# Another order of all engines' steps, with the first two masks on VectorE and g in the raw w_out

## The chip, the cores and the metric

The kernel runs on one core of one Trainium2 chip. The metric is the device time of one execution in microseconds (us). Engines are named as in the profile: PE (TensorE matmuls), PEld (its weight loads), DVE (VectorE), ACT (ScalarE), POOL (GpSimd) and SP (SyncE, which issues the transfers here).

## The reference

Attention over 8 batches, 8 heads, 576 positions and 64 head dimensions, followed by a feed-forward stage over 4608 tokens of 512 values. Each attention output is the sum of two: one on q, k and v averaged over groups of four positions, repeated four times, and one local, in which a position sees only those less than four away.

```
mask = np.abs(pos[:, None] - pos[None, :]) < factor        # factor = 4
out_d = sm_attn(q_d, k_d, v_d)                             # q_d = mean of 4 positions, ...
out_up = np.repeat(out_d, factor, axis=2)
scores = scale * np.matmul(q, k.transpose(0, 1, 3, 2))
scores = np.where(mask, scores, -1000000000.0)
out_local = np.matmul(softmax(scores), v)
x = out_up + out_local                                     # -> (4608, 512)

h = x @ w_in                                               # 512 -> 1024
solu = h * softmax(h)
ln = (solu - mean) / np.sqrt(var + 1e-06) * g_ln
out = ln @ w_out                                           # 1024 -> 512
```

Inputs are float32, the weights float64.

## The kernel before, in words

**Tiles.** The feed-forward stage takes 36 tiles of 128 tokens. A tile i goes through `xhl` (x is split into a rounded high part xh and a low part xl), `ffn_in` (h in two halves of 12 matmuls, line 862: xh with wi_h and wi_l, xl with wi_h; then the maximum `nmx` L870, the exponential L874, the product `e` L877, the mean, the centring L900 or L902, and the write of u to memory), `ffn_back` (u is read back as v, in blocks), `ffn_ut` (two block transposes of v on DVE, L963, then the split into uh on ACT, L969, and ul, L972) and `ffn_out` (o in two halves of 12 matmuls, L986, scaled on ACT, L993, and stored). The last tile, 35, is transposed by PE (`ut`, L959) instead of going through memory. The accumulators of h and of o exist once each: h_(i+1) starts when `e` of tile i has been computed, and o_(i+1) when o_i has been scaled.

**Attention.** A batch is prepared (`prepare`): for batches 0 and 1 q and k are transposed by PE (`qp`, `kp`, L557) and copied (L265, or L263 on ACT); for the others DVE transposes them (L463, L467). DVE sums groups of four into qd and kd (L419). Then there are four `Pooled` units (per pair of heads: scores `sd` L788, maximum L795, exponential, division L812, transpose `pdt` L823, product `po` L844, addition to x L578) and five windows of local attention: `Local` units for batches 0 to 2 and the last window of the others, `PairOfLocals` for the rest. A `Local` unit computes scores `sc` (L607), masks them, subtracts the maximum, exponentiates, divides (L639 to L645), transposes (`plt` L655), multiplies with v (`xp` L665) and adds to x.

**Masks.** In `Local`, a batch below MASKED (2 before) is masked by PE: two bf16 matmuls of the identity with the mask (L600) start the accumulation that the score matmuls continue; DVE then takes the maximum (L620) and subtracts it (L622) straight from the scores. Any other batch is masked by DVE (L625 adds the mask), DVE takes the maximum (L630), and POOL or DVE subtracts it (L632).

**Weights.** They come as float64, as sixteen pieces of 512 KB: 0 to 7 of w_in, 8 to 15 of w_out. A piece is turned into float32 by an absolute value on ACT (L364), a clip on POOL or DVE (L366), and a shift and two combining steps on DVE (L370, L375, L379). It is then rounded into a high part on ACT and a low part. For w_out, `G_LATE` multiplies g in at the rounding (L402) and again in the low part, a fused DVE step (L404).

**Order.** All these steps are numbered in a list `plan`. ORDER is a written-out order of those numbers, by which the instructions of all engines are issued; each engine and the SP queue of transfers runs its own in that order. OTHER lists the steps that go to the second of two engines (POOL or DVE, ACT or DVE). 24 `warm` steps of two matmuls on an idle tile (L1043) are spread over the first part of ORDER.

```
if early:
    for a in range(2):
        nc.tensor.matmul(sc[:, a, ...], ident_b, mask_b..., start=True, stop=False)
...
if early:
    nc.vector.tensor_reduce(out=mx, in_=sc, op=ALU.max, axis=AX.X)
    nc.vector.tensor_tensor(out=pl, in0=sc, in1=max_bc, op=ALU.subtract)
else:
    nc.vector.tensor_tensor(out=pl, in0=sc, in1=mask..., op=ALU.add)
    nc.vector.tensor_reduce(out=mx, in_=pl, op=ALU.max, axis=AX.X)
    engine(nc.gpsimd, nc.vector).tensor_tensor(out=pl, in0=pl, in1=max_bc, op=ALU.subtract)
```

Of the kernel before, what the change touches and what calls it, by code (L numbers as in the profile page):

```python
# [137 lines left out]
def pooled_local_attention_then_solu_ffn(  # L138
# [40 lines left out]
    MASKED = 2  # L179
    WARM = 24  # L180
    SUMS_ON_PE = 0
    G_LATE = True
# [973 lines left out]
```

## Time and profile before

| | |
|---|---|
| median of 3 runs | 602.21 us (599.0 to 603.77) |
| the profiled execution | 600.81 us |
| its span, first to last instruction | 599.0 us |
| mean granted clock of TensorE | 0.996 |
| busy: PE, DVE, ACT, POOL | 567.2, 487.0, 330.7, 285.2 us |
| moved | 99.57 MB, 166 GB/s over the span |
| PE in h (L862) and o (L986), share of the chain that ended last | 25% and 27% |

A row of a group gives line, engine, operation, tiles with shapes and count, then busy time and the mean of one in ns, then the idle time of the engine before these instructions and what ended it. A row of a timeline gives start, duration, engine, line and tiles, and in brackets the idle time before. A matmul's end is modelled, so what a matmul costs PE in a row of them is read from start to start.

### The profile page before, as it was taken

How to read it: one execution, taken by the hardware profiler on the slowest of the kernel's cores; microseconds unless marked ns; L12 is line 12 of the kernel's file. 1: busy time of each engine (PE TensorE's matmuls, PEld its weight loads, DVE VectorE, ACT ScalarE, POOL GpSimd, SP SyncE). 2: the span in 40 equal slices, each digit the busy share in tenths (PEclk: the TensorE clock that was granted, in tenths of full speed). 3: DMA queues.
4: the chain of work that ended last, by engine and by line, in shares of the span. 5: the costliest groups of instructions: out<-in, count | busy, mean ns of one | idle time of the engine just before them, and what ended most of it. 6: DMA issues, size and time to landing. Idle time of an engine off the chain costs nothing.

```text
span 599.0 us, 15199 instructions
## 1 busy us (share of the span) xinstructions
PE 567.2 (95%) x5852; PEld 434.6 (73%) x5852; DVE 487.0 (81%) x792; ACT 330.7 (55%) x743; POOL 285.2 (48%) x433
## 2 busy tenths in 40 slices
PE   6887878999999999999989999999999999999996
PEld 3565556777777777777767877777777777778874
DVE  6999999988988889878897997998788568645540
ACT  4667657267654576456563665456635764243542
POOL 4567577653554666363552155446325643322120
PEclk9999999899999999999999999999999999999999
DMA  8998756778678876887986878776474442332330
GB/s 267 264 224 223 169 130 116 184 161 182 170 194 175 199 172 161 209 178 178 219 175 175 162 194 206 167 177 194 124 202 136 128 148 89 108 135 86 112 124 35
DMA packets 207111, 99.57 MB, mean 166 GB/s; under 512 B 163136, under 2 KB 193344, under 8 KB 207040
## 3 DMA queue, kind: packets, MB, share of 16 engines
q1 hardware_dynamic: 207040, 98.61, 65.4%
q8 instruction: 46, 0.75, 0.5%
q14 instruction: 25, 0.20, 0.1%
HBM read 65.54 MB, written 27.79 MB: 156 GB/s over the span
## 4 chain that ended last, share of the span: by engine, by line
PE 64%; DVE 13%; DMA 7%; issue 4%; POOL 4%; SPq 4%; ACT 3%; DVEq 0%; POOLq 0%; ACTq 0%
PE o L986 27%; PE h L862 25%; PE po L844 2%; PE sd L788 2%; DMA w<-in_moe_w_in_dram 2%; DMA vw<-in_v_dram 2%; DMA qm<-in_q_dram 1%; PE pdt L823 1%; SPq L286 1%; PE xp L753 1%; SPq L305 1%; PE sc L695 1%; PE xp L665 1%; DVE nmx L870 1%; POOL w L366 1%
## 5 line engine op out<-in xcount | busy, mean ns | idle before, releaser
L986 PE MATMUL o<-wo_h,uh 128*128 128x512 f32 x288 | 118.4, 411 | 1.9 <-ACT osb L993 1.6
L862 PE MATMUL h<-wi_h,xh 128*128 128x512 f32 x288 | 115.9, 402 | 1.4 <-DVE e L877 1.2
L862 PE MATMUL h<-wi_h,xl 128*128 128x512 f32 x288 | 114.2, 397 | 0.7 <-POOL xl L1020 0.7
L986 PE MATMUL o<-wo_l,uh 128*128 128x512 f32 x288 | 114.7, 398 | 0.0
L862 PE MATMUL h<-wi_l,xh 128*128 128x512 f32 x288 | 113.6, 394 | 0.0
L986 PE MATMUL o<-wo_h,ul 128*128 128x512 f32 x288 | 79.2, 396 | 1.5 <-POOL ul L972 0.9
L874 ACT ACTIVATE e<-h,nmx 128x1024 f32<-128x1024 f32 x36 | 40.1, 1114 | 53.7 <-DVE nmx L870 53.2
L986 PEld LDWEIGHTS o<-wo_h,uh 128*128 128x128 f32 x288 | 54.5, 189 | 18.6 <-issue 2.8
L870 DVE TENSOR_REDUCE nmx<-h 128x1 f32<-128x1024 f32 x36 | 43.7, 1214 | 29.3 <-PE h L862 29.3
L862 PEld LDWEIGHTS h<-wi_h,xh 128*128 128x128 f32 x288 | 54.0, 188 | 15.6 <-DVE e L877 1.6
L986 PEld LDWEIGHTS o<-wo_h,ul 128*128 128x128 f32 x288 | 54.0, 188 | 15.6 <-DVE ul L972 1.4
L862 PEld LDWEIGHTS h<-wi_h,xl 128*128 128x128 f32 x288 | 54.1, 188 | 14.7 <-POOL xl L1020 1.5
L986 PEld LDWEIGHTS o<-wo_l,uh 128*128 128x128 f32 x288 | 54.7, 190 | 11.8
L862 PEld LDWEIGHTS h<-wi_l,xh 128*128 128x128 f32 x288 | 54.1, 188 | 12.3
L972 POOL TENSOR_TENSOR ul<-v,uh 128x512 fp32r<-128x512 f32 x31 | 40.1, 1299 | 46.4 <-ACT uh L969 37.1
L969 ACT ACTIVATE uh<-v 128x512 fp32r<-128x512 f32 x70 | 43.3, 623 | 29.7 <-DVE v L963 19.9
L877 DVE SCALAR_TENSOR_TENSOR e<-h,e 128x1024 f32<-128x1024 f32 x36 | 43.7, 1214 | 18.0 <-ACT e L874 17.7
L963 DVE STREAM_TRANSPOSE v<-v 128x512 f32<-128x512 f32 x70 | 46.9, 689 | 0.8 <-DMA v<-u 0.7
L993 ACT ACTIVATE osb<-o,s 128x512 f32<-128x512 f32 x36 | 24.5, 680 | 35.6 <-PE o L986 22.2
L882 POOL TENSOR_SCALAR nmu<-su 128x1 f32<-128x1 f32 x36 | 9.3, 257 | 70.3 <-DVE e L877 63.5
L900 ACT ACTIVATE e<-e,nmu 128x1024 f32<-128x1024 f32 x28 | 32.1, 1146 | 16.8 <-POOL nmu L882 16.8
L919 ACT ACTIVATE e<-e 128x1024 f32<-128x1024 f32 x35 | 36.7, 1049 | 2.2 <-DMA u<-e 2.2
(125 smaller groups left out, 1124.6 us busy)
## 6 DMA issues: line engine op xcount, KB each, us to landing
u<-e SPq DMA_DIRECT2D x35, 512.0 KB
v<-u SPq DMA_DIRECT2D x140, 128.0 KB
vs<-in_v_dram SPq DMA_DIRECT2D x32, 288.0 KB
out_dram<-osb SPq DMA_DIRECT2D x36, 256.0 KB
qm<-in_q_dram SPq DMA_DIRECT2D x96, 72.0 KB
km<-in_k_dram SPq DMA_DIRECT2D x96, 72.0 KB
vw<-in_v_dram SPq DMA_DIRECT2D x80, 64.0 KB
vw<-in_v_dram SPq DMA_DIRECT2D x40, 128.0 KB
```

What stands on the lines that cost most here:

```text
L788: nc.tensor.matmul(sd[rows((par + c) % 2), (0, 2, 1)[c], :], qd_flat[rows(par), (NPR - 1 - pr) * SD + c * QN:][:, 0:64], bt.kd[rows(par), ...
L862: nc.tensor.matmul(hps[:, n, :], src[:, cc, :], wt[:, cc, n * 512:(n + 1) * 512], start=(cc == 0 and src is xh and wt is wi_h), stop=(cc = ...
L870: nc.vector.tensor_reduce(out=nmx, in_=hf, op=ALU.max, axis=AX.X, negate=True)
L874: nc.scalar.activation(e, hf, AF.Exp, bias=nmx, scale=1.0, accum_out=se)
L877: nc.vector.scalar_tensor_tensor(out=e, in0=hf, scalar=1.0, in1=e, op0=ALU.mult, op1=ALU.mult, accum_out=su)
L900: nc.scalar.activation(e, e, AF.Identity, bias=nmu, scale=1.0)
L919: nc.scalar.activation(e0, e, AF.Square, accum_out=m2)
L963: nc.vector.transpose(vg, vg)
L969: nc.scalar.activation(uh, tp, AF.Copy)
L972: (usual if v is None else engine(usual, nc.vector)).tensor_tensor(out=ul, in0=tp, in1=uh.bitcast(F32), op=ALU.subtract)
L986: nc.tensor.matmul(o, src[:, j, :], wt[:, 4 * g + j, :], start=(g == 0 and j == 0 and src is uh and wt is wo_h), stop=(g == 1 and j == 3 a ...
L993: nc.scalar.activation(osb, o, AF.Copy, scale=s)
```

## The change

Three constants change, and with them the tables.

```diff
 ORDER = """
-8 0 23 168 169 22 170 171 172 173 174 25 24 10 175 160 161 162 163 164 176 177 16 26 27 32 28
...
+23 16 165 166 2 4 167 168 169 170 171 24 26 27 25 28 29 3 172 33 32 30 31 173 174 197 17 175
...
 OTHER = """
-37 53 59 93 178 186 202 210 242 250 258 266 274 282 471 482 524 541 543 549 566 568 574 643 671
...
+27 78 188 215 220 239 255 276 292 294 437 551 553 576 609 628 651 685 697 709 721 731 738 752
...
     EARLY = 2
-    MASKED = 2
+    MASKED = 0
     WARM = 24
     SUMS_ON_PE = 0
-    G_LATE = True
+    G_LATE = False
     FIRST_ON_PE = ()
```

MASKED = 0 lets all `Local` units of batches 0 and 1 take the branch that the others took: no mask matmuls, the mask added by DVE, and one step more each (ten in all), the subtraction, on POOL or DVE. The matrices ident_b and mask_b are gone, and the warm-up matmuls use a zeroed tile `filler` that POOL writes. G_LATE = False multiplies g into the float32 piece of w_out by an ACT step of its own, after which the piece is rounded and its low part taken as for w_in, on POOL or DVE:

```
nc.scalar.activation(t, t, AF.Copy, scale=g)
...
nc.scalar.activation(hi, t, AF.Copy)
yield
engine(nc.gpsimd, nc.vector).tensor_tensor(out=lo, in0=t, in1=hi.bitcast(F32), op=ALU.subtract)
```

Lines of the changed file are one lower than before (L624 is the old L625). OTHER has 115 entries, not 133. By its and ORDER's doing DVE has, over the whole program: 13 clips, not 6; four low parts of weights, and no fused ones (8); 20 mask adds of `Local`, not 10; 9 xl, not 19; 35 ul, not 41; 8 pairs of sums of v, not 10; 2 wide subtractions and 2 wide multiplications of `PairOfLocals`, not 3 and 4. What DVE gives up of these goes to POOL. In the SP queue the first transfers are a piece of w_in, q, k, k, q, and the second piece, where they were a piece, k, q, and the second piece.

The first scores on PE, before: `sc_1` and `sc_2` are windows 1 and 2 of batch 0.

```order
L823 MATMUL pdt_0_406<-ident,pd_0_318 72x64 x12
L600 LDWEIGHTS ident_b
L600 MATMUL sc_1_422<-mask_b,ident_b 128x256
L600 LDWEIGHTS ident_b
L600 MATMUL sc_1_422<-mask_b,ident_b 128x256
L607 MATMUL sc_1_422<-kT_171,qT_170 64x64 x16
```

And now, where windows 0 and 1 come first:

```order
L606 MATMUL sc_0_378<-kT_151,qT_150 64x64 x16
L606 MATMUL sc_1_395<-kT_151,qT_150 64x64 x16
L822 MATMUL pdt_0_412<-ident,pd_0_246 72x64 x12
L1042 LDWEIGHTS filler
L1042 MATMUL warm_442<-filler 128x512
```

Each unit's pair of mask matmuls is gone, and the score matmuls start the accumulation themselves.

DVE shortly before the first h, before: `w_10` and `w_8` are pieces of w_out, `sc_0` window 0 of batch 1, `pl` the local scores.

```order
L370 TENSOR_SCALAR w_10_944<-w_10_944 128x512
L366 TENSOR_SCALAR w_8_1003<-w_8_1003 128x512
L375 SCALAR_TENSOR_TENSOR w_10_944<-w_10_875,w_10_944 128x512
L620 TENSOR_REDUCE mxl_0_1033<-sc_0_1007 128x8
L379 SCALAR_TENSOR_TENSOR w_10_944<-w_10_875,w_10_944 128x512
L370 TENSOR_SCALAR w_8_1003<-w_8_1003 128x512
L622 TENSOR_TENSOR pl_108<-sc_0_1007,mxl_0_1033 128x4x128
L375 SCALAR_TENSOR_TENSOR w_8_1003<-w_8_904,w_8_1003 128x512
L404 SCALAR_TENSOR_TENSOR wo_l<-w_10_944,g_sb,wo_h 128x512
```

And now, with the same window and piece 8, and the low part of tile 0's x (`xl`), which POOL computed before:

```order
L624 TENSOR_TENSOR pl_106<-sc_0_933,mask 128x4x128
L365 TENSOR_SCALAR w_8_965<-w_8_965 128x512
L629 TENSOR_REDUCE mxl_0_950<-pl_106 128x8
L369 TENSOR_SCALAR w_8_965<-w_8_965 128x512
L374 SCALAR_TENSOR_TENSOR w_8_965<-w_8_957,w_8_965 128x512
L794 TENSOR_REDUCE mxd_0_990<-sd_0_974 128x3
L1019 TENSOR_TENSOR xl_988<-x_559,xh_987 128x512
L378 SCALAR_TENSOR_TENSOR w_8_965<-w_8_957,w_8_965 128x512
L631 TENSOR_TENSOR pl_106<-pl_106,mxl_0_950 128x4x128
```

The mask add, the maximum and the subtraction stand where a maximum and a subtraction stood, and no fused low part (L404) is left; this subtraction is the only one of batches 0 and 1 that DVE keeps.

DVE ahead of the transposes of tile 1's v (`v_1796`, later `v_1852`), on which o_1 waits, before: `x_1517` is x of batch 1, `sc_0` window 0 of batch 2.

```order
L625 TENSOR_TENSOR pl_109<-sc_0_1730,mask 128x4x128
L404 SCALAR_TENSOR_TENSOR wo_l<-w_14_1560,g_sb,wo_h 128x512
L404 SCALAR_TENSOR_TENSOR wo_l<-w_15_1474,g_sb,wo_h 128x512
L630 TENSOR_REDUCE mxl_0_1747<-pl_109 128x8
L265 COPY x_1517<-xp_4_1775 128x4x112
L870 TENSOR_REDUCE nmx_1793<-h_1640 128x1
L265 COPY x_1517<-xp_3_1757 128x4x116
L578 TENSOR_TENSOR x_1517<-x_1517,po_1_1751 128x576
L419 TENSOR_REDUCE qd_flat<-qT_1496 128x144
L578 TENSOR_TENSOR x_1517<-x_1517,po_0_1853 128x576
L963 STREAM_TRANSPOSE v_1796<-v_1796 128x4x128 x2
```

And now:

```order
L378 SCALAR_TENSOR_TENSOR w_14_1782<-w_14_1305,w_14_1782 128x512
L624 TENSOR_TENSOR pl_105<-sc_2_1758,mask 128x4x128
L577 TENSOR_TENSOR x_1438<-x_1438,po_0_1846 128x576
L411 TENSOR_TENSOR wo_l<-w_13_1705,wo_h 128x512
L794 TENSOR_REDUCE mxd_0_1881<-sd_0_1874 128x3
L418 TENSOR_REDUCE qd_flat<-qT_1552 128x144
L577 TENSOR_TENSOR x_1438<-x_1438,po_3_1893 128x576
L624 TENSOR_TENSOR pl_106<-sc_3_1901,mask 128x4x128
L629 TENSOR_REDUCE mxl_0_1686<-pl_107 128x8
L418 TENSOR_REDUCE qd_flat<-qT_1552 128x144 x2
L962 STREAM_TRANSPOSE v_1852<-v_1852 128x4x128 x2
```

Four mask adds of batch 2 instead of two, a maximum of its pooled scores (`mxd`) and all four of its sums qd instead of one now stand ahead of these transposes; the copies of batch 1's x have gone to ACT, and the maximum of the fourth h (`nmx`) has moved behind.

201 rows, old and new, of tables (ORDER, OTHER) are left out of this document.

## The prediction

> **What bounds the kernel now.** I read the page's engine totals, then stages by windows, then what TensorE (PE) waits for in each.
>
> ```profile
> span 599.0 us, 15199 instructions
> PE 567.2 (95%) x5852; PEld 434.6 (73%) x5852; DVE 487.0 (81%) x792; ACT 330.7 (55%) x743; POOL 285.2 (48%) x433
> 0.00:20.00 20.00, 14.06 (x176) 8.32 (x176) 15.04 (x28) 8.58 (x14) 7.66 (x14) 1.00 0.93 278
> 20.00:120.00 100.00, 83.61 (x1347) 60.69 (x1346) 96.99 (x158) 61.62 (x153) 70.03 (x63) 0.98 0.77 181
> 120.00:150.00 30.00, 30.00 (x276) 22.95 (x274) 25.49 (x47) 20.31 (x48) 14.18 (x24) 1.00 0.78 172
> 150.00:200.00 50.00, 49.29 (x599) 38.38 (x599) 45.62 (x79) 26.09 (x54) 27.96 (x45) 1.00 0.78 182
> 120.00:580.00 460.00, 456.10 (x4273) 355.41 (x4272) 371.90 (x603) 254.91 (x568) 206.22 (x352) 1.00 0.65 163
> ```
>
> The columns after the length are PE, PEld, DVE (VectorE), ACT, POOL, then clock, DMA share, GB/s. There are two stages. Up to 120 us DVE is the bound: 112.0 us busy of 120, and 97.0 of the 100 from 20 on, while PE fills holes with its warm-up matmuls. From 120 to 580 PE is: 456.1 of 460. So time is won or lost in three ways: how early DVE has the first tiles ready, how much PE work is left from there, and the few PE waits after it, which are these:
>
> ```profile
> PE h L862 <- DVE e L877: 1.2, 1, 1.2
> PE o L986 <- DVE ul L972: 0.7, 1, 0.7
> PE sc L695 <- ACT pdT L263: 0.7, 2, 0.5
> PE xp L665 <- DVE pl L701: 0.6, 1, 0.6
> ```
>
> **The change part by part.** The twenty mask matmuls go. Two of them hold PE for 26.85 - 26.52 = 0.33 us, so ten units hold it 3.3 us.
>
> ```profile
> 26.52 0.39 PE L600 MATMUL sc<-mask_b,ident_b 128*128 128x256 bf16 x2
> 26.85 0.69 PE L607 MATMUL sc<-kT,qT 64*64 64x64 f32 x32
> 27.48 0.39 PE L600 MATMUL sc<-mask_b,ident_b 128*128 128x256 bf16 x2
> ```
>
> All of them run in the first stage, where PE waits for DVE anyway, so by themselves they are worth 0; 3.3 us is the other end, if that cover is gone. On DVE the ten units trade one pair for another of equal cost, and the subtraction goes to POOL (nine times) or DVE (once):
>
> ```profile
> L625 DVE TENSOR_TENSOR pl<-sc,mask 128x512 f32<-128x512 f32 x10 | 6.7, 682 | 0.4 <-PE sc L607 0.4
> L622 DVE TENSOR_TENSOR pl<-sc,mxl 128x512 f32<-128x512 f32 x10 | 6.7, 676 | 0.0
> ```
>
> What decides the first stage is therefore the DVE queue. I take the transposes of tile 1's v as the mark, since o_1 starts right behind them (124.20) and PE hardly waits again. Counted in the instruction order, 174 DVE instructions stand ahead of them before and 182 now, the setup at the very start left out. By kind, with these rows:
>
> ```profile
> L366 DVE TENSOR_SCALAR w<-w 128x512 f32<-128x512 f32 x6 | 4.5, 758 | 3.2 <-ACT w L364 3.2
> L404 DVE SCALAR_TENSOR_TENSOR wo_l<-w,g_sb,wo_h 128x512 fp32r<-128x512 f32 x8 | 5.8, 738 | 0.0
> L972 DVE TENSOR_TENSOR ul<-v,uh 128x512 fp32r<-128x512 f32 x39 | 29.3, 751 | 8.2 <-ACT uh L969 7.6 <-POOL s L926 0.2
> L419 DVE TENSOR_REDUCE qd_flat<-qT 128x144 f32<-128x576 f32 x32 | 23.6, 736 | 0.1
> L870 DVE TENSOR_REDUCE nmx<-h 128x1 f32<-128x1024 f32 x36 | 43.7, 1214 | 29.3 <-PE h L862 29.3
> ```
>
> Seven more clips (6 to 13): 7 x 0.758 = +5.3. Eight fused low parts go, -8 x 0.738 = -5.9; four of the sixteen plain ones come to DVE, which the trace lacks there, at the like subtraction L972, 4 x 0.751 = +3.0 (one ScalarE multiply more per w_out piece is hidden: ACT is busy 62 of those 100 us). Six instructions of batch 2 are pulled ahead of the mark (two mask adds, three qd sums, one maximum), about 0.7 each: +4.2. Fifteen others, seven added and eight dropped, the dearest a dropped nmx of 1.214, come to about -2.2 by the means of the same view. Sum +4.4 us on DVE. In return PE has done more by then, two sd, two sc and one po, 0.64, 0.63 and 0.64 each by the starts quoted (sc above, the others below), 3.2 us, and two warm-up steps of 0.56 are still to run, 1.1 us.
>
> ```profile
> 121.78 0.60 PE L1043 MATMUL warm<-ident_b 128*128 128x512 bf16 x2
> 122.34 1.29 PE L607 MATMUL sc<-kT,qT 64*64 64x64 f32 x64
> 124.20 0.49 PE L986 MATMUL o<-wo_h,uh 128*128 128x512 f32 x1
> 127.20 0.71 PE L844 MATMUL po<-pdT,vd 72*64 72x144 f32 x8
> 127.84 0.71 PE L788 MATMUL sd<-kd,qd_flat 64*64 64x144 f32 x12
> 128.48 0.49 PE L986 MATMUL o<-wo_h,uh 128*128 128x512 f32 x1
> ```
>
> First stage: +4.4 - 3.2 + 1.1 = **+2.3 us**. Its ends: clips at 0.417 or 1.124 (quoted below) instead of 0.758, -2.4 to +2.6, and the masks in full, -3.3.
>
> First loads: the second weight piece is now the sixth transfer in the sync queue, not the fourth, behind two more head loads of 288 KB. At the 278 GB/s of the first window that is 2.1 us, for a DVE that already waited for that piece:
>
> ```profile
> 8.94 1.11 DVE L366 TENSOR_SCALAR w<-w 128x512 f32<-128x512 f32 x1 [1.27 <-ACT w L364]
> ```
>
> DVE now has a copy and a sum of batch 0 to do in between, so I take **+1.0**, ends 0 and 2.1.
>
> Behind the first stage DVE loses work to POOL: 10 of 19 xl, 6 of 41 ul, 2 of 10 vsum pairs, 3 of 7 wide subtract and multiply steps. POOL, 206 us busy of 460, has room. The waits quoted above (1.2, 0.7, 0.7, 0.6: 3.2 us) can go; another order makes others, so half: **-1.6**, ends -3.2 and 0.
>
> One new tight place: xl_31 moves from DVE to POOL, and x of it is finished only by the po just ahead of o_28's second half:
>
> ```profile
> L1020 POOL TENSOR_TENSOR xl<-x,xh 128x512 fp32r<-128x512 f32 (+1 forms) x21 | 27.5, 1311 | 13.3 <-ACT xh L1017 13.0
> L1020 DVE TENSOR_TENSOR xl<-x,xh 128x512 fp32r<-128x512 f32 (+1 forms) x19 | 12.0, 639 | 3.4 <-ACT xh L1017 3.2
> ```
>
> That is 0.67 us longer against 2.8 us of matmuls that must cover it: **+0.5**, ends 0 and 1.3. The tail: the two transposes of tile 35 stood on both sides of o_34, two breaks of 0.94 and 1.86 us; now they stand together behind o_34, one break of about 1.86: **-0.9**.
>
> ```profile
> 580.70 0.60 PE L959 MATMUL ut<-ident,v 128*128 128x128 f32 x4
> 581.64 0.51 PE L986 MATMUL o<-wo_h,uh 128*128 128x512 f32 x1 [0.34 <-ACT osb L993]
> 587.35 0.60 PE L959 MATMUL ut<-ident,v 128*128 128x128 f32 x4
> 589.21 0.51 PE L986 MATMUL o<-wo_h,uh 128*128 128x512 f32 x1 [1.26 <-ACT osb L993]
> ```
>
> Sum: 2.3 + 1.0 - 1.6 + 0.5 - 0.9 = +1.3. The profiled execution took 600.81 us (span 599.0, 1.8 around it), so the changed kernel comes to 602.1; the median of the runs, 602.21, lies 1.4 above that execution. Forecast 602, no change.
>
> [...] DVE and POOL get in each other's way in this trace: the shift L370 has one form and yet these extremes, and the clip likewise (0.417 to 1.124).
>
> ```profile
> L366 DVE TENSOR_SCALAR w<-w x6: 417/740/1124, 5.3 to 62.4; 128x512 f32<-128x512 f32 x6
> L370 DVE TENSOR_SCALAR w<-w x16: 383/427/1523, 5.8 to 105.2; 128x512 int32<-128x512 int32 x16
> ```
>
> [...]
>
> The clock also has its row: 115 to 120 us.
>
> ```profile
> 115.00:120.00 5.00, 4.75 (x37) 3.83 (x37) 4.97 (x8) 0.06 (x1) 3.40 (x4) 0.66 0.69 166
> 113.91 0.93 PE L665 MATMUL xp<-plT,vw 64*64 64x58 f32 x38 [0.98 <-DVE pl L625]
> 115.87 4.54 PE o L986 x12
> 137.14 2.80 PE o L986 x12
> ```
>
> Twelve matmuls took 4.54 us where twelve others take 2.80: 1.7 us lost after waits of 1 us. [...]
>
> **The rivals.** *Faster.* The masks were not hidden: POOL and DVE keep ahead, PE gets its 3.3 us, clips run at 0.417 (-2.4), all 3.2 us of late waits go (-1.6 more), loads and xl_31 cost nothing (-1.5): 602.1 - 8.8 = 593.3. For it: DVE gives up work in sum and batch 2's loads are issued earlier. Against: 97% DVE in that stage and a longer queue.
>
> *Slower.* DVE's arrears last. Between 120 and 200 us DVE idled 4.5 + 4.4 = 8.9 us, free because it was ahead of PE. If the queue that is 4.4 us longer is not worked off there, each such idle microsecond is one of PE: 602.1 + 8.9 = 611.0 if all of it, 606.5 if half; over 1% slower once some two thirds are paid. For it: batch 2 and the last w_out piece (13) are still in the queue. Against: PE holds 12 matmuls for 2.80 us, 48 a tile, while the DVE steps of a tile are few.
>
> [...]
>
> **How the numbers follow.** About 1% (6.0 us) is what a measurement of this kernel tells from no change. Forecast 0.42 (602.1) and lock 0.08 (604.7), both within 1%; faster 0.27 (593.3); slower 0.23 (606.5 to 611). The range 593 to 611 takes in all four prices; what lies outside is a stall in the new order that no row shows. The forecast's own ends are 597.2 (masks -3.3, late waits -1.6 more) and 606.3 (clips +2.6, late waits +1.6).
>
> **What would show it.** Right: DVE again 95% or more busy from 20 us on, PE's steady stage beginning 1 to 4 us later, h_0 not earlier than before, fewer DVE releasers of PE after 280 us. Faster rival: o_1 starting before 123 us. Slower: PE waits for DVE of several us between 125 and 200. [...] I am wrong altogether if PE waits for loads (vw_1_4 or w_out piece 13, both late in the sync queue), or if POOL releases PE often.

## The result and the profile after

The changed kernel took 593.64 us (median of 4 runs, 591.93 to 594.66) beside 601.17 for the kernel before: ratio 0.987, 95% interval 0.9821 to 0.9919. Timed twice more, it gave 0.9883 (0.9849 to 0.9917) and 0.9892 (0.9857 to 0.9927). It is 1.1 to 1.3% faster. The range of the prediction held the time; its likeliest case, no change at 602, did not come true, and the time is that of the rival called faster (593.3), but not for that rival's reasons, as the experiments show: the closeness of the two numbers is in part luck.

The profiled execution took 594.66 us. First its span and engine totals from the page, then its stages by windows (columns as in the prediction):

```profile
span 592.8 us, 15179 instructions
PE 568.5 (96%) x5832; PEld 439.3 (74%) x5832; DVE 468.1 (79%) x769; ACT 335.9 (57%) x751; POOL 317.8 (54%) x465
0.00:20.00 20.00, 15.33 (x156) 9.58 (x158) 14.20 (x24) 8.19 (x18) 6.34 (x15) 0.97 0.94 265
20.00:120.00 100.00, 88.65 (x1463) 66.20 (x1460) 93.34 (x167) 72.53 (x173) 71.95 (x69) 0.92 0.87 192
120.00:150.00 30.00, 30.00 (x233) 22.86 (x233) 28.22 (x51) 19.60 (x46) 22.23 (x36) 1.00 0.78 182
150.00:200.00 50.00, 47.51 (x551) 37.13 (x550) 45.15 (x70) 29.13 (x68) 31.12 (x41) 1.00 0.73 168
200.00:580.00 380.00, 378.83 (x3402) 297.40 (x3401) 285.69 (x458) 201.76 (x442) 184.66 (x300) 1.00 0.61 159
```

From 20 to 120 us DVE is 93.3 us busy, not 97.0, although its queue is longer, and the mean clock is 0.92, not 0.98. From 120 to 200 DVE has less slack in sum than before (28.2 and 45.2 busy, against 25.5 and 45.6), and PE, which idled 0.7 us from 150 to 200, now idles 2.5. Behind 200 us PE hardly waits. These are the waits of PE from 200 us to the end, all of them, in the changed kernel:

```profile
PE h L861 <- POOL xl L1019: 1.2, 2, 0.9
PE o L985 <- ACT uh L968: 0.7, 1, 0.7
```

Before, the same view gives the 1.2, 0.7 and 0.6 shown in the prediction, 0.2 twice, and the tail's

```profile
PE o L986 <- ACT osb L993: 1.6, 2, 1.3
PE o L986 <- ACT uh L969: 0.3, 1, 0.3
```

together 4.8 us against 1.9.

Breaks too short for that list count too, so I also kept PE's account. Each matmul that still has to start is given the mean start-to-start time of its line behind 125 us in both kernels' traces (h 238 ns, o 240, po 80, sd 49, plt 117, pdt 38, sc and xp 18; qp and kp 54, masks 158 and warm 292 by their own). What is left of the time up to the last matmul is loss. The account is good to about 1 us; the last two columns bear the argument.

| kernel | last matmul at | work left at 200 us | loss from 120 to 200 | loss behind 200 |
|---|---|---|---|---|
| before | 594.7 | 388.9 | 1.3 | 5.8 |
| clips_dve | 597.4 | 391.6 | 1.1 | 5.9 |
| g_early | 600.4 | 394.4 | 2.8 | 6.0 |
| new_then_old | 592.8 | 386.5 | 2.0 | 6.3 |
| after, three traces | 588.5, 584.1, 588.6 | 387.5, 383.0, 387.5 | 2.8, 2.5, 2.8 | 1.0, 1.1, 1.1 |
| masks_on | 590.3 | 390.9 | 4.0 | -0.5 |
| trim | 587.9 | 387.0 | 6.3 | 0.8 |
| old_then_new | 600.9 | 401.4 | 14.1 | -0.5 |
| clips_pool | 609.4 | 407.8 | 9.5 | 1.6 |

Of the 6.2 us between the two profiled spans, 1.4 were won by 200 us and 4.8 behind it. In the second trace of the changed kernel it is 5.9 and 4.7: the later part repeats, the first stage varies from run to run.

A stretch at half clock (0.50 granted) counts as loss here too, with up to half its length. After 120 us there is one in *trim* (183.6 to 187.0 us), in *old_then_new* (139.2 to 146.0), in *clips_pool* (128.1 to 134.9) and in *masks_on* (up to 122.4): up to 1.7, 3.4, 3.4 and 1.2 us of their losses from 120 to 200.

### The profile page after: what moved, and what is told of

It reads as the page before. It is cut to its first block, busy times and chain, and to the rows that moved or that the text cites. A ratio compares the mean times of both kernels' runs of the same rounds, so it can differ in the third digit from the quotient of the medians.

```text
span 592.8 us, 15179 instructions
## 1 busy us (share of the span) xinstructions
PE 568.5 (96%) x5832; PEld 439.3 (74%) x5832; DVE 468.1 (79%) x769; ACT 335.9 (57%) x751; POOL 317.8 (54%) x465
## 4 chain that ended last, share of the span: by engine, by line
PE 72%; DVE 10%; SPq 4%; DMA 4%; issue 4%; POOL 3%; ACT 2%; DVEq 0%; POOLq 0%; ACTq 0%
PE h L861 28%; PE o L985 27%; SPq L285 3%; PE sd L787 2%; PE po L843 2%; PE xp L752 2%; PE pdt L822 2%; PE kp L556 2%; PE warm L1042 2%; PE qp L556 1%; PE sc L694 1%; DMA qm<-in_q_dram 1%; DMA u<-e 1%; POOL xl L1019 1%; PE sc L606 1%
## 5 line engine op out<-in xcount | busy, mean ns | idle before, releaser
L985 PE MATMUL o<-wo_h,uh 128*128 128x512 f32 x288 | 116.4, 404 | 0.8 <-ACT uh L968 0.7
L971 POOL TENSOR_TENSOR ul<-v,uh 128x512 fp32r<-128x512 f32 x37 | 48.3, 1312 | 24.7 <-ACT uh L968 20.9
L1019 POOL TENSOR_TENSOR xl<-x,xh 128x512 fp32r<-128x512 f32 (+1 forms) x31 | 37.6, 1219 | 16.5 <-ACT xh L1016 16.0
L899 ACT ACTIVATE e<-e,nmu 128x1024 f32<-128x1024 f32 x29 | 33.3, 1148 | 19.7 <-POOL nmu L881 19.7
```

The source lines that it names most:

```text
L899: nc.scalar.activation(e, e, AF.Identity, bias=nmu, scale=1.0)
L971: (usual if v is None else engine(usual, nc.vector)).tensor_tensor(out=ul, in0=tp, in1=uh.bitcast(F32), op=ALU.subtract)
L985: nc.tensor.matmul(o, src[:, j, :], wt[:, 4 * g + j, :], start=(g == 0 and j == 0 and src is uh and wt is wo_h), stop=(g == 1 and j == 3 a ...
L1019: engine(nc.gpsimd, nc.vector).tensor_tensor(out=l, in0=src, in1=h.bitcast(F32), op=ALU.subtract)
```

## Experiments

### Are the mask matmuls worth anything?

*unmasked*: the mask matmuls are left out of the kernel before.

```diff
-            if early:
-                for a in range(2):
-                    nc.tensor.matmul(
-                        sc[:, a, 0:NPR * W]..., ident_b,
-                        mask_b..., start=True, stop=False,
-                    )
...
-                        start=not early, stop=not early or pr == NPR - 1,
+                        start=True, stop=True,
```

> The kernel before in its own order, with the twenty mask matmuls left out and nothing put in their place (the local scores of batches 0 and 1 stay unmasked, so the output differs there). Theory M: TensorE gets 3.3 us back, ratio 0.9945. Theory Q, VectorE's queue covers them: 1.000, between 0.998 and 1.002.

Measured: 602.42 us, ratio 1.004 (1.0013 to 1.0068). Nothing is won; if anything 2 us are lost. In this kernel's trace the granted clock is 0.94 from 20 to 120 us, where it was 0.98, but three traces of the changed kernel alone differ by as much (0.92 to 0.97), so that this comes from the masks is not shown.

*masks_on*: the changed kernel with its masks back on PE.

```diff
-    MASKED = 0
+    MASKED = 2
```

> The changed kernel in its new order, with the masks of batches 0 and 1 back on TensorE (MASKED = 2), the maximum and the subtraction at the places of the mask add and the maximum, and no GpSimd subtraction for them. Theory M: the 3.3 us come back, ratio to the kernel before 0.9925 (the changed kernel has 0.987). Theory Q: the masks are free here too, 0.987; the gain is the order's.

Measured: 594.18 us, 0.9895 (0.987 to 0.992), where the changed kernel has 0.9883 and 0.9892. No gain from leaving the masks out of PE can be seen in the new order either, though *masks_on* also spares POOL the nine subtractions, which could cover a small one. Theory M falls; the prediction's 0 stands.

*masks_off*: the kernel before with its masks on DVE.

```diff
-    MASKED = 2
+    MASKED = 0
```

> The kernel before, in its own order, with MASKED = 0 alone: the twenty mask matmuls are gone, VectorE adds the mask and takes the maximum at the places where it took the maximum and subtracted, and the subtraction follows at once (nine on GpSimd, one on VectorE). Theory M, the masks' 3.3 us were on TensorE's path in the first stage: about 3.3 us faster, ratio 0.9945, TensorE's loss before 120 us as in the kernel before. Theory Q, the VectorE queue sets the end of the first stage and covered them: ratio 1.000, the loss before 120 us 3 us larger. If the added GpSimd step between the maximum and the exponential delays the local units: slower, 1.002 to 1.005.

In this kernel the mask add of batch 0's window 4 writes the buffer from which window 0 still reads, so the output of these two windows differs, and part of its time may come from that. Measured: 618.56 us, 1.0303 (1.0274 to 1.0333), far outside what either theory gave. Waits of GpSimd (POOL) and of DVE up to 140 us:

```profile
POOL pl L632 <- DVE mxl L630: 19.2, 7, 4.8
DVE w L370 <- POOL w L366: 9.2, 6, 4.9
```

POOL stood 19.2 us before the added subtractions, the clips that follow them in its order came late, and DVE, which needs the clips, waited 9.2 us for them (2.3 before).

### Where in the order does the gain lie?

*new_then_old*: the new flags and order up to the first half of h_4, behind it what is left in the old order; *old_then_new*: the reverse, with the old flags. The tables part at these numbers:

```diff
 359 354 896 886 892 341 342 535
-756 377 710 693 694 713 902 727
+1 12 317 756 377 757 713 701
...
 336 717 337 377 355 356 548 525
-526 357 358 748 527 667 359 736
+881 736 737 738 667 766 739 767
```

> The changed kernel with its flags, in its new order up to the first half of h of tile 4 (128 us), behind it in the order of the kernel before. Theory M plus an unchanged loss in the first stage: 3.0 us faster than the kernel before, ratio 0.995. Theory L alone (all the gain is later): 1.000. If the first stage's order is itself the gain and the seam costs nothing: 0.990 or less.

Measured: 599.11 us, 0.9961 (0.9938 to 0.9985).

> The kernel before with its flags, in its own order up to the first half of h of tile 4 (131 us), behind it in the order of the changed kernel, as far as steps are left. Theory L, the later order is worth the waits it removes (in the traces TensorE loses 5.5 us between 120 and 580 us before, 3.2 after, and 1.0 less in the tail): ratio 0.9945. If the new later order pays only behind the new first stage: 1.000 or slower.

Measured: 606.71 us, 1.0093 (1.0068 to 1.0118). The seams may cost something, but what happens behind 200 us is plain. The largest waits of PE there, first of new_then_old, then, all of them, of old_then_new:

```profile
PE o L986 <- ACT osb L993: 1.6, 2, 1.3
PE h L862 <- DVE e L877: 1.6, 2, 1.2
PE o L986 <- DVE ul L972: 0.7, 1, 0.7
PE xp L665 <- DVE pl L701: 0.6, 1, 0.6
```

```profile
PE o L985 <- ACT uh L968: 0.7, 1, 0.7
PE h L861 <- POOL xl L1019: 0.2, 1, 0.2
```

The late waits go with the late order, whatever came ahead of it: every trace of the table with the old one loses 5.8 to 6.3 us behind 200 us, every trace with the new one at most 1.6. (By the same account *unmasked* and *masks_off*, with the old one, lose about 6 and 7, and *warm_early*, with the new one, about 1.) Order here includes the engine choices that come with it, the xl, ul and sums of v that went to POOL; the two were not tried apart. A kernel with the old order up to tile 12 and the new one behind it deadlocks and has no time, so the gain was not narrowed down further either. From the new first stage to the whole new order the time falls from 0.9961 to 0.988, some 4.7 us with an uncertainty of 2.5. The first stage with its seam brings the 2.3 us of new_then_old (0.9 to 3.7). What old_then_new loses lies at its seam, 14.1 us between 120 and 200: 10.7 in waits, most of them of sd, sc and h for ScalarE (ACT) and DVE, and up to 3.4 in the half clock named above.

### What sets the first stage?

*clips_dve* and *clips_pool* exchange the two kernels' shares of the clips; *g_early* sets one flag and gives two of the eight plain low parts of w_out to DVE. In this order:

```diff
-178 186 202 242 258 266 274 282
+234
...
-239
+183 191 207 247 263 271 279 287
...
-    G_LATE = True
+    G_LATE = False
+271 287
```

> The kernel before, order and flags untouched, with seven clips of weight pieces moved from GpSimd to VectorE (13 and 3, the split of the changed kernel). In the trace of before GpSimd's ten clips of 1.99 us lie beside four of VectorE's 54 weight steps and stretch them by 0.4 us in all, while its two-tensor steps stretch others by some 12 us. Theory V, VectorE's busy time up to the mark sets the first stage: seven clips at 0.43 to 0.76 us are 3 to 5 us slower, ratio 1.005 to 1.009. Theory C, GpSimd's clips are what stretches VectorE's weight steps: stretch falls from 12 to about 6 us, 1 to 3 us faster, ratio 0.995 to 0.998.

Measured: 604.11 us, 1.0056 (1.0038 to 1.0074), as theory V has it. The transposes of tile 1's v come 3.0 us later (125.58), with DVE 2.1 us busier up to them; the granted clock fell too, to 0.90 from 20 to 120 us, where it was 0.98; whether the last 0.9 us are its doing was not settled. The stretch of the weight steps (how it is summed stands in the next section) stays at 11.0 us, so theory C falls.

> The changed kernel in its order, with ten clips on GpSimd and six on VectorE, the split of the kernel before. Theory V: VectorE is 3 to 5 us less busy and the first stage that much shorter, ratio to the kernel before 0.979 to 0.983 (the changed kernel has 0.988). Theory C: the stretch of VectorE's weight steps grows from 6 to about 12 us, ratio 0.993 to 0.998. If GpSimd's queue (13 us fuller) delays the local units' subtractions and multiplications instead: slower than 0.995 without more stretch.

Measured: 612.03 us, 1.0197 (1.0173 to 1.0222): 18.5 us slower than the changed kernel, far beyond every case given. The stretch did grow to 13.1 us, but DVE is also 9 us less busy from 20 to 120 us (84.3), and that gained nothing. DVE's largest wait up to 135 us says why:

```profile
DVE w L369 <- POOL w L365: 10.4, 8, 2.7
```

The granted clock was lower as well (0.83, where it was 0.92); its share of the loss was not settled.

> The kernel before, order and masks untouched, with G_LATE = False alone: the eight fused low parts (5.9 us) leave VectorE, which gets two plain ones (1.5 us), GpSimd six of about 1.3 us, ScalarE eight multiplications more. Theory V: 4.4 us faster, ratio 0.9927. If GpSimd's six two-tensor steps stretch VectorE's steps by what they relieve: 0.998 to 1.002.

Measured: 609.37 us, 1.0131 (1.0108 to 1.0154). Neither case: DVE's busy time from 20 to 120 us falls by 11 us to 85.8, and the kernel is 8 us slower. The largest wait of PE and two of DVE there:

```profile
PE h L862 <- POOL xl L1020: 6.1, 1, 6.1
DVE nmx L870 <- PE h L862: 7.1, 1, 7.1
DVE w L370 <- POOL w L366: 4.6, 3, 3.6
```

The low parts that POOL now computes stand ahead of tile 0's xl, for which the first h waits those 6.1 us, and of clips, and POOL itself waits for ACT's rounding before it can start them:

```profile
65.93 1.26 POOL L412 TENSOR_TENSOR wo_l<-w,wo_h 128x512 fp32r<-128x512 f32 x1 [4.10 <-ACT wo_h L410]
67.15 1.72 POOL L1020 TENSOR_TENSOR xl<-x,xh 128x512 fp32r<-128x512 f32 x1
```

So theory V is only half right: more on DVE costs time, but less on DVE gains none where it is put into POOL's queue without another order. Each part of the change that was put alone into the old order made the kernel slower, or at best no faster.

### The clock and the last tight places

*warm_early*: six warm steps earlier. *trim*: two warm steps earlier, and two steps on which PE waits between 160 and 180 us later. The numbers of *trim* that move:

```diff
 77 78 42
+12 1
...
-742
 609 720
+742
...
-972 973
 573 574 569 570 554
+972 973
```

> The changed kernel with six of its 24 warm steps moved: from 86.2 to 148.3 us, where TensorE is at its full clock, to the gaps at 15, 18, 20.5 and 42.5 us, ahead of the two places where the granted clock fell to 0.5 (18.9 to 32.7 and 46 to 49.5 us). If the half clock delays the keys and scores that VectorE waits for there (waits of 0.37, 0.61, 0.80 and 2.03 us behind it) and the two last steps cost TensorE 0.56 us each: 1.1 to 5 us faster than the changed kernel, ratio to before 0.979 to 0.985, granted clock near 0.995. If neither is on the path: 0.987.

Measured: 593.3 us, 0.9867 (0.9825 to 0.991). The half clock moved more than it went (16 to 20 and 33 to 40 us, where the changed kernel's trace has 19 to 32 and 46 to 50), and the time stayed.

> The changed kernel with three moves in its order: the two last warm steps (132.6 and 148.3 us, where TensorE has no gap, 0.56 us each) go to the gap at 20.5 us; the scores sd and their maximum of pair 1 of batch 3 go behind the first half of o_4, ahead of which TensorE waited 1.29 us for the mask add at 177 us; the transposes plt of window 4 of batch 2 go behind a product xp, where they waited 0.68 us at 166 us for ScalarE. If what TensorE does and waits for behind 120 us goes into the time one to one: 3.1 us faster than the changed kernel, the loss behind 120 us down from 3.7 to about 1.7 us, ratio to the kernel before 0.983. If other waits take their place: 0.988.

Measured: 594.16 us, 0.9914 (0.9883 to 0.9946), beside 593.55 for the changed kernel. Its waits of PE behind 120 us hold new ones:

```profile
PE h L861 <- DVE e L876: 1.6, 1, 1.6
PE xp L664 <- DVE pl L700: 1.0, 1, 1.0
PE sc L694 <- DVE qT L466: 0.7, 1, 0.7
```

The loss from 120 to 200 us rose from 2.8 to 6.3: PE's listed waits there from 2.5 to 3.8, and up to 1.7 is the half clock at 183.6 us. Masks, warm steps and single tight places of PE all gained nothing up to 200 us. That a wait for DVE takes their place is what the new waits suggest; it is not shown for each. No kernel tried here is measurably faster than the changed one, whose two repetitions were expected so:

> The changed kernel as it is, timed beside the next three and the kernel before: about 593.6 us, ratio 0.987. It is the measure for masks_on (0.9895) too: if it comes to 0.9895, the masks are worth nothing in the new order; 0.984 would make them worth their 3.3 us.

Measured: 593.29 us, 0.9883 (10 runs, 590.25 to 598.76).

> The changed kernel once more, as the measure for the kernel above: 593.5 us, ratio 0.988, and a loss of 3.7 us behind 120 us as in its two other traces.

Measured: 593.55 us, 0.9892.

## Why the likeliest case was wrong, step by step

**Masks, 0.** Right, for the reason given, by *unmasked* and *masks_on*. The 3.3 us of the faster rival were not what made its time come true.

The forecast was +1.3 us, the profiled execution came 6.2 lower: 7.5 apart. By the account 4.7 of them lie in the first stage with the first loads (+3.3 forecast, -1.4 measured at 200 us) and 2.8 behind (-2.0 forecast, -4.8 measured).

**First stage, +2.3.** This is the step that failed first. The mark, tile 1's transposes, comes at 121.30 us, 1.3 earlier (116.85 and 121.39 in the two other traces), and o_1 at 122.75; by 200 us 1.4 us are won. What failed is the sum +4.4 on DVE. Up to the mark, by windows that end there, DVE has 193 instructions, not 187, yet is busy 108.84 us, not 112.74: -3.9 (-4.3 and -1.5 in the two others). The counts were right and the fused low parts' -5.9 too; the four low parts cost 3.3 (3.0 forecast). The durations were not constants. Weight steps on DVE before, then after:

```profile
L375 DVE SCALAR_TENSOR_TENSOR w<-w,w 128x512 int32<-128x512 int32 x12 | 10.4, 865 | 0.1
L370 DVE TENSOR_SCALAR w<-w 128x512 int32<-128x512 int32 x16 | 13.1, 821 | 2.5 <-POOL w L366 2.3
```

```profile
L374 DVE SCALAR_TENSOR_TENSOR w<-w,w 128x512 int32<-128x512 int32 x12 | 9.2, 763 | 0.2
L369 DVE TENSOR_SCALAR w<-w 128x512 int32<-128x512 int32 x16 | 10.0, 627 | 0.3
L365 DVE TENSOR_SCALAR w<-w 128x512 f32<-128x512 f32 x13 | 7.3, 559 | 2.0 <-ACT w L363 2.0
```

The thirteen clips took 7.3 us, so seven more cost 2.8, not 5.3. The 48 shifts and combining steps, which the change does not touch and the sum left out, went from 39.2 to 33.5. These two make up 8.2 of the 8.3 us by which the sum is off. The cause is what stands on POOL at the same moment, as here before, POOL first:

```profile
78.51 1.29 POOL L1020 TENSOR_TENSOR xl<-x,xh 128x512 fp32r<-128x512 f32 x1
79.75 1.09 POOL L812 TENSOR_TENSOR pd<-pd,rsd 128x432 f32<-128x432 f32 x1
```

```profile
78.58 1.50 DVE L370 TENSOR_SCALAR w<-w 128x512 int32<-128x512 int32 x1 [0.79 <-POOL w L366]
80.00 1.39 DVE L379 SCALAR_TENSOR_TENSOR w<-w,w 128x512 int32<-128x512 int32 x1
```

Over fourteen traces no weight step without a POOL instruction beside it took longer than 0.43 us (clip, shift: 169 steps) or 0.69 us (the two others: 232). Beside two-tensor steps of POOL they took up to 1.5 and 1.8, and two of them, in *g_early* and *masks_off*, 2.9 and 3.9. Their time above 0.43 and 0.69 adds up to 12.3 us in the trace of before and to 10.4 to 12.4 in five others with the old first stage (*clips_dve* and *g_early* among them), but only to 5.2 to 8.5 in seven with the new one.

The steps beside POOL's did not become fewer: 22 of 54 weight steps before and 20 of 61 after began while a two-tensor step of POOL was running. What changed is how much of POOL's step was then left: 0.83 us on the average before, 0.39 after. In the fourteen traces 284 weight steps began so, and 263 of them took longer by just that rest less 0.14 us, to within 0.1 us; most of the others met a POOL step that was itself held up, or a second one behind it. Weight steps that began ahead of POOL's were not stretched (at most 0.01 us in each trace). The new order, then, lets DVE's steps begin later in POOL's. That POOL was busier from 20 to 120 us, 72.0 us instead of 70.0, did not make DVE's weight steps slower. *clips_pool*, the new order with other clips, has 13.1 again, so it is order and engines together.

That DVE's 3.9 us gave only 1.4 by 200 us has two likely parts: the half clock (17 us of it in this trace, below), and 1.5 us more loss of PE from 120 to 200 us, where batch 2's steps are still queued on DVE. That loss is the mechanism of the rival called slower, and its size was 1.5 us, not 4.5 to 8.9. How much the clock took was not settled.

**First loads, +1.0.** Not to be seen: up to 20 us DVE was busy 14.20, 15.14 and 14.86 us in three traces of the changed kernel and 15.04 before, which is between 0.1 more and 0.8 less.

**Late waits, -1.6; xl_31, +0.5; tail, -0.9.** The signs were right and the sum too small. Of the 2.9 us of list waits in the stage, the 1.2, 0.7 and 0.6 shown, 0.2 and 0.2, all went: -2.9, near the end of -3.2 that I halved on the thought that another order makes others. It made one of 0.94 us, at 478 us, where POOL's xl took 2.73 us instead of 1.29, and 0.23 us at xl_31. The tail's waits fell from 1.9 to 0.7. The list makes it -2.9 in all, the account -4.8; the 1.9 between them are breaks too short to be listed, or the account's error.

**Clock, not in the sum.** What it cost the changed kernel was not measured. The half clock at 115 us went, and longer stretches came, 17 us at half clock in this trace and 10 in the two others:

```profile
15.00:20.00 5.00, 2.83 (x38) 2.04 (x38) 4.77 (x5) 3.27 (x12) 3.34 (x3) 0.88 1.06 247
20.00:25.00 5.00, 2.76 (x36) 2.47 (x34) 4.84 (x10) 3.02 (x11) 0.00 (x0) 0.50 1.00 227
25.00:30.00 5.00, 5.00 (x62) 3.94 (x62) 4.56 (x9) 2.69 (x6) 3.21 (x3) 0.50 1.06 240
```

**The signs named.** DVE at 95% or more: 93.3, and 96.5 and 95.0 in the two other traces. h_0 not earlier: 65.38, not 61.16, but 60.25 and 60.4 in the two other traces. Waits for DVE of several us from 125 to 200, the sign of the slower rival: 1.3 and 0.5. The 604.7 us that the prediction calls lock have the seven added clips at 1.124 us each, which no run shows: the thirteen of the changed kernel took 0.559 us on average, with a median of 0.427. o_1 before 123 us, the sign of the faster rival, came. Fewer DVE releasers late: yes. PE waited for no weight, and for POOL 1.2 us late.

## What to carry to other kernels

The durations here belonged to their neighbours: 263 of the 284 weight steps on DVE that began while a two-tensor step of POOL was running took their undisturbed time (up to 0.43 or 0.69 us) plus what was left of POOL's step less 0.14 us, to within 0.1 us. Where a trace shows that, price a step so, not by the mean of a few. A new order and the choices of engine that it was written for are one change; its parts, tried alone in another order, say little about the whole. Look for a new order's gain in the last stage too, where nothing behind can swallow a wait that goes.

## What was not expected of the hardware

The granted clock's half-speed stretches (0.50) lasted one to four times 3.41 us in these traces (13.65 and 3.41 in that of after). In the trace of after PE ran matmuls for 1.5 of the 3.4 us ahead of the first of them (18.8 us), and in the trace of before for 2.0 of the 3.4 ahead of the one at 115.8 us. Yet in that same trace PE ran them for only 0.61 us from 83.25 to 86.66 us, and the clock was 1.00 from 80 to 90. What starts such a stretch was not shown.

In ten runs of the changed kernel the mean clock and the time went together (0.991 with 590.25 us, 0.979 with 598.76, correlation -0.92), yet six more runs show no such tie (correlation +0.26), and *warm_early* had 0.993 on average and the same median. Whether the clock makes the time or both follow the first loads stays open.

POOL's clip, a step of 1.92 us (median, before and after) with one input tensor, stretched DVE's weight steps by at most 0.4 us, and only those that began in its first 0.4 us: of 43 that began during one, the 20 with at most 1.35 us of it left were not stretched. Single two-tensor steps of 1.1 to 1.5 us stretched them by up to 1.1.
